# Low parts of 18 token-weight pieces added up by GpSimd's transfers instead of subtracted on VectorE and GpSimd

## The chip, the core and the metric

One NeuronCore of a Trainium2 chip runs the whole program. Its engines are TensorE (PE in the profile; PEld is its weight load), VectorE (DVE), ScalarE (ACT), GpSimd (POOL) and SyncE (SP), which issues all transfers of the kernel before. The metric is the device time of one execution in microseconds (us); lower is better.

## What is computed

The reference is three blocks in a row, on 8 batches of 576 tokens with 512 channels:

```
# attention with keys and values averaged over groups of 8 tokens
attn = softmax(q @ mean8(k).T / 8) @ mean8(v)            # 8 heads of 64
# mixing with a phase
theta = x @ w_theta
y = w_tok_r @ (x * cos(theta)) + w_tok_i @ (x * sin(theta))
u = x + y;  x = u + relu(u @ w_ch)
# token MLP, then channel MLP
u = x + w_tok2.T @ relu(w_tok1.T @ x);  out = u + relu(u @ w_ch1) @ w_ch2
```

The weights arrive in 64-bit floating point. What this case is about is how `w_tok` (the real and the imaginary token weights on top of each other, 9 blocks of 128 rows x 576 columns) becomes two float32r halves for TensorE: a high part, the weight rounded to float32r, and a low part, the weight minus the high part. A product is then high x high + high x low + low x high.

## The kernel before

Batch 0 and the conversion of the weights run side by side in the first 110 us, written by a planner (`first_batches`, class `Plan`). Each operation has one or more ways (engine, estimated ns, a mark, a function), dependencies and homes in SBUF. `Plan.run` simulates the plan once by rank and then in 400 random changes of the priorities with a fixed seed, keeps the best, and emits the operations in that order. After that `Arrange` sorts the instructions of the whole program once more, each engine's on its own, by prices (`price`) and lags (`depend`). So an altered operation or estimate can alter the order of everything around it.

`add_piece` converts one piece. There are 26: pieces 0 to 7 are `w_theta` (256 columns each), pieces 8 to 25 `w_tok`: first the 9 blocks' columns 0 to 287, then their columns 288 to 575. SP loads the 64-bit words into a tile named `early`; ACT writes the absolute value, scaled, into a slot (`absf`, L2254); VectorE shifts it (`shl`, L2258), sets the sign (`sign`, L2262) and the lowest bits (`low3`, L2267), which leaves the weight in fp32. For a token piece ACT then rounds it into the high part (`hi`, L2282), `w()[:, 0]`, and VectorE (for even pieces, `LOWS`) or GpSimd (for odd ones) subtracts the high part into the low part, `w()[:, 1]` (`low`, L2285). The slots are 7 (`mids`: `cvt0`, 3 of `zt1` and 3 of `vr`, seen as cvt and early in the profile); a slot is given back when both `hi` and `low` have read it, and the next `absf` waits for it.

TensorE uses the pieces in the mixing of batch 0: for each half of the channels two groups of columns 0 to 255 (128x256 products) and two of columns 256 to 575 (128x320). A group is 27 products into one bank, `m0` or `m1`: the 9 high parts, the 9 low parts, and the 9 high parts again with the low part of Z. So the last token pieces are wanted when the first 128x320 group begins. A bank is emptied by VectorE (`R<-m`), and the next group of the bank waits for that.

While TensorE would idle before the first mixing product, the planner puts in filler products (`busy`); after it none.

## Time and profile before

| | |
|---|---|
| time, median of 3 runs (lowest to highest) | 1228.55 us (1228.24 to 1229.01) |
| the profiled execution: its time, its span | 1229.43 us, 1227.7 us |
| TensorE busy, instructions | 1218.7 us (99%), 7980 |
| weight loads busy | 1184.0 us (96%) |
| VectorE busy, instructions | 1040.5 us (85%), 1873 |
| ScalarE busy, instructions | 708.2 us (58%), 1467 |
| GpSimd busy, instructions | 320.1 us (26%), 395 |
| transfers | all on SP's queue, 225.42 MB |

The shares are over the whole span. A busy TensorE is one that has a product in flight, and a product that waits in the array counts as busy too, so stretches are better compared by what they contain: so many products of a shape, at the pace that a dense row of them has (the next row's start minus this row's start, over their number), against the time that they took. The granted clock of a stretch, PEclk, is 1.00 at full speed. The records count an fp32 product as two.

### The profile page before, as it was taken

Reading aid. Unit: us, or ns where it says so; the run is one execution under the profiler, and the core shown is the slowest. Engines: PE = TensorE matmul, PEld = TensorE weight load, DVE = VectorE, ACT = ScalarE, POOL = GpSimd, SP = SyncE. Lnnn points to the kernel's source line nnn. Section 1 sums busy time; section 2 is a strip of 40 time slices with the busy share of each in tenths; the row PEclk is TensorE's granted clock in tenths of the full one; section 3 lists DMA queues with packets and bytes.
Section 4 is the critical chain, followed back from the end, with each engine's and each line's share of the span. In section 5 each row is a group of like instructions: output and inputs, shape, how many; then the busy total and the mean of one; then the engine's idle time right before and its main releaser. Section 6 shows DMA issues by size and latency. Waiting matters only on the chain.

```text
span 1227.7 us, 22986 instructions
## 1 busy us (share of the span) xinstructions
PE 1218.7 (99%) x7980; PEld 1184.0 (96%) x7980; DVE 1040.5 (85%) x1873; ACT 708.2 (58%) x1467; POOL 320.1 (26%) x395
## 2 busy tenths in 40 slices
PE   9999999999999999999999999999999999999998
PEld 5889999999999999999999999999999999999998
DVE  7988879899898967999999859889963799998894
ACT  6878776776857664544445456676654543443442
POOL 2152434535253533000012100122100033134113
PEclk9999999999999999999999999999999999999999
DMA  9523335554433466534358887787769867546622
GB/s 332 173 96 125 119 116 159 145 149 128 159 115 97 128 178 206 189 101 130 112 161 227 275 286 247 245 294 258 250 214 330 295 205 251 168 136 225 214 77 77
DMA packets 193556, 226.88 MB, mean 185 GB/s; under 512 B 72992, under 2 KB 147232, under 8 KB 193440
## 3 DMA queue, kind: packets, MB, share of 16 engines
q1 hardware_dynamic: 193440, 225.42, 57.0%
q8 instruction: 63, 1.03, 0.4%
q14 instruction: 53, 0.43, 0.1%
HBM read 140.55 MB, written 84.80 MB: 184 GB/s over the span
## 4 chain that ended last, share of the span: by engine, by line
PE 90%; DVE 4%; DMA 3%; ACT 1%; issue 1%; SPq 0%; POOL 0%; ACTq 0%; DVEq 0%; POOLq 0%
PE m L437 32%; PE x L437 31%; PE t L437 23%; PE x L451 3%; DMA early<-w_tok 1%; DMA con<-consts 1%; DMA raw_n<-scr_x 1%; DMA early<-w_theta 0%; SPq L2160 0%; DVE tmp L2727 0%; DVE early L2267 0%; PE t L451 0%; PE m L451 0%; DMA pool<-pool 0%; DVE early L2262 0%
## 5 line engine op out<-in xcount | busy, mean ns | idle before, releaser
L437 PE MATMUL m<-wtk,Z 128*128 128x320 f32 (+1 forms) x1536 | 254.8, 301 | 1.6 <-ACT wtk L2282 1.4
L437 PEld LDWEIGHTS m<-wtk,Z 128*128 128x128 f32 x1536 | 220.0, 190 | 3.8 <-ACT wtk L2282 2.1
L1901 POOL TENSOR_TENSOR o<-o,u 128x384 f32<-128x384 f32 x12 | 17.6, 1479 | 234.2 <-DVE u L1889 181.1
L1052 POOL TENSOR_TENSOR Z<-tmp,Z 128x1024 fp32r<-128x1024 f32 x26 | 63.2, 2442 | 44.3 <-ACT Z L1051 44.3
L437 PE MATMUL t<-wth,Xh 128*128 128x256 f32 x432 | 60.7, 282 | 0.1
L437 PE MATMUL x<-ope_Xh,wa 128*128 128x384 f32 x288 | 60.2, 337 | 0.0
L437 PE MATMUL x<-ope_Z,wa 128*128 128x384 f32 x300 | 60.0, 337 | 0.0
L437 PE MATMUL m<-wtk,zt 128*128 128x256 f32 (+1 forms) x192 | 57.3, 299 | 0.0
L437 PEld LDWEIGHTS t<-wth,Xh 128*128 128x128 f32 x432 | 55.9, 188 | 0.8 <-DVE tmp L2683 0.3
L437 PE MATMUL x<-ope_Xl,wa 128*128 128x384 f32 x252 | 54.6, 336 | 0.0
L1425 POOL TENSOR_TENSOR wo<-wm,wo 128x256 fp32r<-128x256 f32 (+1 forms) x24 | 17.8, 742 | 138.5 <-ACT wo L1424 121.9
L437 PE MATMUL m<-ope_Z,wa 128*128 128x384 f32 x252 | 53.3, 337 | 0.0
L437 PEld LDWEIGHTS x<-ope_Z,wa 128*128 128x128 f32 x300 | 53.3, 188 | 0.0
L437 PE MATMUL t<-ope_Z,wa 128*128 128x384 f32 x252 | 53.1, 337 | 0.0
L437 PEld LDWEIGHTS x<-ope_Xh,wa 128*128 128x128 f32 x288 | 51.2, 188 | 0.0
L437 PE MATMUL x<-ope_R,wa 128*128 128x384 f32 x240 | 47.3, 337 | 0.3 <-ACT ope_R L1648 0.3
L437 PEld LDWEIGHTS x<-ope_Xl,wa 128*128 128x128 f32 x252 | 44.9, 188 | 0.0
L437 PEld LDWEIGHTS t<-ope_Z,wa 128*128 128x128 f32 x252 | 44.8, 188 | 0.0
L437 PEld LDWEIGHTS m<-ope_Z,wa 128*128 128x128 f32 x252 | 44.6, 188 | 0.0
L437 PEld LDWEIGHTS x<-ope_R,wa 128*128 128x128 f32 x240 | 42.2, 188 | 0.7 <-ACT ope_R L1648 0.6
L437 PE MATMUL x<-bdk,q 128*128 128x144 f32 x292 | 40.9, 287 | 0.0
L437 PE MATMUL x<-opo_Z,wa 128*128 128x384 f32 x216 | 40.6, 336 | 0.0
(476 smaller groups left out, 3634.1 us busy)
## 6 DMA issues: line engine op xcount, KB each, us to landing
wa<-scr_w SPq DMA_DIRECT2D x42, 512.0 KB, 5.3
scr_g<-g SPq DMA_DIRECT2D x108, 192.0 KB, 3.2
scr_u<-R SPq DMA_DIRECT2D x32, 288.0 KB, 2.2
u<-scr_u SPq DMA_DIRECT2D x32, 288.0 KB, 4.4
scr_x<-u SPq DMA_DIRECT2D x32, 288.0 KB, 2.1
raw_n<-scr_x SPq DMA_DIRECT2D x24, 384.0 KB, 4.8
scr_w<-wo SPq DMA_DIRECT2D x36, 256.0 KB, 3.7
o<-scr_x SPq DMA_DIRECT2D x48, 192.0 KB, 3.0
```

The costliest lines, as they stand in the source:

```text
L437: nc.tensor.matmul(out=o, lhsT=l, rhs=r, start=start, stop=stop, skip_group_check=skip)
L451: nc.tensor.transpose(o, i, ident)
L1052: later(1.0 if lo is nc.vector else 0.0, lambda: lo.tensor_sub(out=zl, in0=zv, in1=zh.bitcast(F32)), tg, zg)
L1425: eng.tensor_sub(out=o[:, :, 1], in0=src, in1=o[:, :, 0].bitcast(F32))
L1901: nc.gpsimd.tensor_tensor(out=u22[d].t, in0=u22[d].t, in1=u2[d].t, op=ALU.add)
```

## The change

For the 18 token pieces (`DMAS`) the low part is made otherwise. ACT writes minus the weight into the low part's place (`negative`, which rounds as `hi` does), and GpSimd issues a transfer from the slot to that place which adds what it carries to what stands there (`accumulate`). The slot is given back when `hi` has read it and the transfer has landed. The 9 subtractions on VectorE and the 9 on GpSimd go; 18 ACT instructions and 18 transfers come. The planner is told 1000 ns for the issue and 2500 ns more to the end of such a transfer, `Arrange` 1500 and 3000 ns. These are settings by which it sorts.

```
--- before.py
+++ after.py
@@ -64,6 +64,7 @@
 TRIES = 400
 SEED = 2
 LOWS = range(0, 26, 2)
+DMAS = range(8, 26)
 WS = (1, 2)
 ZL = (1, 1, 1)
 EDVE = (2, 3)
@@ -80,6 +81,7 @@
     SIZE = {"float32": 4, "float32r": 4, "uint32": 4, "bfloat16": 2, "int64": 8}
     TABLE = 1380.0
     LANDING = 1750.0
+    SOFT, SOFT_LANDING = 1500.0, 3000.0
     BEGIN, FIRST, COLD = 750.0, 2600.0, 5000.0
     PACED, LEAD = "ew_", 250e3
     AFTER, MARGIN, RATE, WINDOW = 100e3, 800.0, 300.0, 2500.0
@@ -153,6 +155,8 @@
             return n * 0.833 + (62.0 if ps else 112.0) + (75.0 if len(ins) > 1 else 0.0) + (
                 92.0 if len(outs) > 1 else 0.0), False, table
         if e == "Pool":
+            if op == "DMACopy":
+                return self.SOFT, False, None
             if op == "Memset":
                 return n * 0.9 + 3.0, False, None
             if op == "TensorCopy":
@@ -228,6 +232,8 @@
                 c = self.cost[j]
                 if self.eng[j] == "SP":
                     lag = c[0] + c[1] / (490.0 if c[2] else 262.0) + self.LANDING + self.LAT[e]
+                elif self.eng[j] == "Pool" and self.ins[j].opcode == "DMACopy":
+                    lag = c[0] + self.SOFT_LANDING + self.LAT[e]
                 elif e == "PE" == self.eng[j] and self.acc[i][0][0]["name"] == self.acc[j][0][0]["name"]:
                     lag = c[0]
                 else:
@@ -1962,7 +1968,7 @@
             for o in reversed(self.ops):
                 i = o["i"]
                 e, ns, kb = o["ways"][0][0:3]
-                own = 430.0 + kb * 1024.0 / 262.0 + 1750.0 if e == "SP" else ns + self.TAIL[e]
+                own = 430.0 + kb * 1024.0 / 262.0 + 1750.0 if e == "SP" else ns + self.TAIL[e] + (2500.0 if kb == "dma" else 0.0)
                 self.rank[i] = own + max([0.0] + [self.rank[k] + self.LAT[self.ops[k]["ways"][0][0]] for k in self.after[i]])
 
         def trial(self, prio):
@@ -2041,13 +2047,13 @@
                     if w[2] is True:
                         s = max(s, lock)
                         lock = s + d
-                    elif w[2] and w[2] != table:
+                    elif w[2] and w[2] != "dma" and w[2] != table:
                         s += self.TABLE
                         table = w[2]
                     if e == "PE" and s < 5000.0:
                         d *= 1.7
                     free[e] = s + d
-                    end = s + d + self.TAIL[e]
+                    end = s + d + self.TAIL[e] + (2500.0 if w[2] == "dma" else 0.0)
                 out.append((s, i, w, slot))
                 for g in o["give"]:
                     h = held[id(g)]
@@ -2284,7 +2290,18 @@
             def low(eng):
                 return lambda: eng.tensor_sub(out=w()[:, 1, c0:c1], in0=m_(), in1=w()[:, 0, c0:c1].bitcast(F32))
 
+            def negative():
+                nc.scalar.activation(out=w()[:, 1, c0:c1], in_=m_(), func=ACTF.Copy, scale=-1.0)
+
+            def accumulate():
+                nc.gpsimd.dma_start(out=w()[:, 1, c0:c1], in_=m_(), accum_op=ALU.add)
+
             x = add(("ACT", acs(n), False, hi), [o], hs + [w], give=[hold])
+            if i in DMAS:
+                y = add(("ACT", acs(n), False, negative), [o], hs + [w])
+                y = add(("POOL", 1000.0, "dma", accumulate), [y], hs + [w], give=[hold])
+                conv[what[:3]] = (x, y)
+                return
             ways = [("POOL", po(n), True, low(nc.gpsimd))]
             if i in LOWS:
                 ways = [("DVE", dv(n), True, low(nc.vector))]
```

The order moves with it. GpSimd, from its last softmax copies of batch 0 to the end of the token pieces; `wtk0` to `wtk8` are the blocks, `DMASW` the counters of its own transfers. Before:

```order
L2449 MEMSET vbl_483 128x512 [waits PE_49]
L2285 TENSOR_TENSOR wtk1_485<-early8_359,wtk1_485 128x288 [waits DMAHW2_49,DVE_49,Activation_49]
L2285 TENSOR_TENSOR wtk3_571<-cvt0_287,wtk3_571 128x288 [waits DMAHW6_49,DVE_49,Activation_49]
L2285 TENSOR_TENSOR wtk5_500<-early7_291,wtk5_500 128x288 [waits DVE_49,Activation_49]
L2285 TENSOR_TENSOR wtk7_582<-early8_359,wtk7_582 128x288 [waits Activation_49]
L2285 TENSOR_TENSOR wtk0_542<-early8_359,wtk0_542 128x288 [waits DMAHW0_49,Activation_49]
```

Now, the last eight of the 18 and what follows:

```order
L2297 DMA wtk3_436<-early8_360 128x288 [waits DMASW2_49,Activation_49]
L2297 DMA wtk0_563<-early8_360 128x288 [waits DMASW3_49,Activation_49]
L2297 DMA wtk4_577<-early7_289 128x288 [waits DMASW4_49,Activation_49]
L2297 DMA wtk2_447<-cvt0_285 128x288 [waits DMASW5_49,Activation_49]
L2297 DMA wtk5_528<-early7_289 128x288 [waits DMASW6_49,Activation_49]
L2297 DMA wtk6_569<-early7_289 128x288 [waits DMASW7_49,Activation_49]
L2297 DMA wtk7_572<-early8_360 128x288 [waits DMASW0_49,Activation_49]
L2297 DMA wtk8_567<-early8_360 128x288 [waits DMASW1_49,Activation_49]
L2761 TENSOR_TENSOR Z1_800<-tmp0_771,Z1_800 128x2x512 [waits DMAHW3_49,DMAHW2_49,DMAHW4_49,DMAHW1_49,DMAHW6_49,DMAHW0_49,Activation_49]
```

All 18 transfers stand in GpSimd's one queue ahead of the low parts of Z for the second half.

ScalarE, the last conversions of token pieces. Before, each conversion of a token piece waits for VectorE:

```order
L2254 ACTIVATE early7_291<-early5_252 128x288 [waits DMAHW1_49,DVE_49]
L2282 CAST wtk5_500<-early8_359 128x288 [waits DVE_49]
L2282 CAST wtk0_542<-early8_359 128x288 [waits DVE_49]
L2757 CAST wth2_749<-wt0_390 128x512
L2254 ACTIVATE early8_359<-early6_261 128x288 [waits DMAHW5_49,DVE_49]
L2282 CAST wtk1_485<-early7_291 128x288 [waits DVE_49]
L2282 CAST wtk2_487<-early7_291 128x288 [waits DVE_49]
```

Now (L2260 is `absf`, L2294 `negative`, L2288 `hi`):

```order
L2294 ACTIVATE wtk2_447<-cvt0_285 128x288 [waits DVE_49]
L2294 ACTIVATE wtk5_528<-early7_289 128x288 [waits DVE_49]
L2288 CAST wtk2_447<-cvt0_285 128x288
L2260 ACTIVATE early8_360<-early6_258 128x288 [waits DMAHW5_49,DMASW2_49,Activation_49]
L2294 ACTIVATE wtk6_569<-early7_289 128x288 [waits DVE_49]
L2294 ACTIVATE wtk7_572<-early8_360 128x288 [waits DVE_49]
L2288 CAST wtk5_528<-early7_289 128x288
L2288 CAST wtk6_569<-early7_289 128x288
L2294 ACTIVATE wtk8_567<-early8_360 128x288 [waits DVE_49]
```

`negative` stands ahead of `hi`, and the last piece's `absf` waits for a transfer (DMASW2 is here that of `wtk3`, columns 288 to 575) in place of VectorE.

TensorE, the first 128x320 group. Before, one group runs through alone:

```order
L437 MATMUL m1_764<-wtk7_582,Z0_562 128x320 [waits Activation_49]
L437 MATMUL m1_764<-wtk8_451,zt0_620 128x320 [waits Activation_49]
L437 MATMUL x2_791<-bdk_83,q0_275 128x144 [waits DMAHW7_49,DVE_49,PE_49]
L437 MATMUL x2_791<-bdk_83,q0_275 128x144
L437 MATMUL m1_764<-wtk0_542,Z0_562 128x320 [waits Pool_49]
L437 MATMUL m1_764<-wtk1_485,Z0_562 128x320 [waits DVE_49]
```

Now 17 products of the second group (`m0`) and the scores of batch 1 (`bdk`) stand among the 9 products with low parts, of which these are some:

```order
L443 MATMUL m1_781<-wtk1_504,Z0_565 128x320 [waits DMASW1_49]
L443 MATMUL m0_849<-wtk0_563,Z0_565 128x320 [waits DVE_49]
L443 MATMUL m0_849<-wtk1_504,Z0_565 128x320
L443 MATMUL m1_781<-wtk2_447,Z0_565 128x320 [waits DMASW5_49]
L443 MATMUL x1_810<-bdk_83,q0_292 128x144 [waits DVE_49,PE_49]
L443 MATMUL x1_810<-bdk_83,q0_292 128x144
L443 MATMUL m1_781<-wtk3_436,Z0_565 128x320 [waits DMASW2_49]
```

A low part is thus wanted later than 9 products after its high part.

## Rows read from the trace of the kernel before

**Rows 1.** the windows view: each stretch's busy time by engine, PEclk, DMA share, GB/s.

```profile
53.40:58.80 5.40, 5.40 (x47) 5.40 (x47) 5.27 (x17) 4.05 (x10) 0.00 (x0) 1.00 0.00 0
58.80:61.90 3.10, 3.10 (x11) 1.42 (x10) 3.10 (x9) 2.67 (x7) 2.16 (x2) 1.00 0.00 0
61.90:65.50 3.60, 2.19 (x14) 1.74 (x12) 3.60 (x9) 1.42 (x5) 1.24 (x2) 1.00 0.00 0
...
67.00:69.40 2.40, 2.40 (x12) 2.40 (x11) 2.40 (x4) 1.96 (x4) 0.37 (x1) 0.50 0.37 102
69.40:72.40 3.00, 3.00 (x19) 3.00 (x19) 2.92 (x6) 2.65 (x4) 0.83 (x1) 0.83 0.27 102
```

**Rows 2.** the timeline of TensorE: start, us, instruction, count, idle time and its releaser.

```profile
58.88 3.60 PE L437 MATMUL x<-nat_v,pool 128*128 128x512 f32 x8
61.91 1.44 PE L437 MATMUL m<-wtk,Z 128*128 128x320 f32 x6
...
65.51 0.78 PE L437 MATMUL m<-wtk,Z 128*128 128x320 f32 x2 [1.42 <-ACT wtk L2282]
...
72.49 1.32 PE L437 MATMUL m<-wtk,Z 128*128 128x320 f32 x8
...
73.80 1.03 PE L437 MATMUL m<-wtk,Z 128*128 128x320 f32 x6
74.68 0.90 PE L437 MATMUL x<-bdk,q 128*128 128x144 f32 x6
75.32 0.56 PE L437 MATMUL m<-wtk,Z 128*128 128x320 f32 x2
...
76.25 1.21 PE L437 MATMUL m<-wtk,Z 128*128 128x256 f32 x8
```

**Rows 3.** the instructions of L2285, the subtractions: ns min/median/max, first and last start.

```profile
L2285 DVE TENSOR_TENSOR wtk<-early,wtk x8: 444/451/874, 35.3 to 66.3; 128x288 fp32r<-128x288 f32 x8
L2285 POOL TENSOR_TENSOR wtk<-early,wtk x8: 798/865/1590, 44.7 to 66.4; 128x288 fp32r<-128x288 f32 x8
```

**Rows 4.** the timeline of VectorE around the last pieces.

```profile
52.37 1.24 DVE L2285 TENSOR_TENSOR wtk<-early,wtk 128x288 fp32r<-128x288 f32 x2
...
60.93 0.72 DVE L2267 SCALAR_TENSOR_TENSOR early<-early,early 128x288 uint32<-128x288 uint32 x1
61.57 0.90 DVE L2258 TENSOR_SCALAR early<-early 128x288 uint32<-128x288 uint32 x1
62.39 0.91 DVE L2258 TENSOR_SCALAR cvt<-cvt 128x288 uint32<-128x288 uint32 x1
63.22 0.30 DVE L2258 TENSOR_SCALAR early<-early 128x288 uint32<-128x288 uint32 x1
...
65.29 0.44 DVE L2267 SCALAR_TENSOR_TENSOR early<-early,early 128x288 uint32<-128x288 uint32 x1
65.65 0.67 DVE L2672 SCALAR_TENSOR_TENSOR tmp<-tmp,x 128x512 f32<-128x512 f32 x1
```

**Rows 5.** the timeline of GpSimd at the same place.

```profile
59.74 3.40 POOL L2285 TENSOR_TENSOR wtk<-early,wtk 128x288 fp32r<-128x288 f32 x3 [6.81 <-ACT wtk L2282]
```

**Rows 6.** the timeline of ScalarE: three casts of a token piece in a row.

```profile
45.18 1.09 ACT L2282 CAST wtk<-early 128x288 fp32r<-128x288 f32 x3
```

**Rows 7.** the transfers by issue: count, KB each, median us from issue to landing.

```profile
scr_w<-ew_b SPq DMA_DIRECT2D x48, 128.0 KB, 3.3
...
early<-w_tok SPq DMA_DIRECT2D x14, 288.0 KB, 6.5
...
scr_t<-ew_a SPq DMA_DIRECT2D x5, 128.0 KB, 1.9
```

**Rows 8.** the start: TensorE's fillers and first scores, ScalarE's wait.

```profile
2.30 4.14 PE L447 MATMUL m<-busy 128*128 128x512 bf16 x11 [2.30 <-POOL busy L442]
6.28 1.39 PE L437 MATMUL x<-bdk,q 128*128 128x144 f32 x10
...
14.89 0.95 ACT L2382 ACTIVATE e<-t,mx 128x72 f32<-128x72 f32 x4 [1.96 <-DVE mx L2371]
```

More of the change, by code (lines that the diff above doesn't have):

```diff
@@ L66 @@
 LOWS = range(0, 26, 2)
+DMAS = range(8, 26)
 WS = (1, 2)
@@ L82 @@
     LANDING = 1750.0
+    SOFT, SOFT_LANDING = 1500.0, 3000.0
     BEGIN, FIRST, COLD = 750.0, 2600.0, 5000.0
@@ L155, in price @@
         if e == "Pool":
+            if op == "DMACopy":
+                return self.SOFT, False, None
             if op == "Memset":
@@ L230, in depend @@
                     lag = c[0] + c[1] / (490.0 if c[2] else 262.0) + self.LANDING + self.LAT[e]
+                elif self.eng[j] == "Pool" and self.ins[j].opcode == "DMACopy":
+                    lag = c[0] + self.SOFT_LANDING + self.LAT[e]
                 elif e == "PE" == self.eng[j] and self.acc[i][0][0]["name"] == self.acc[j][0][0]["name"]:
@@ L1964, in prepare @@
                 e, ns, kb = o["ways"][0][0:3]
-                own = 430.0 + kb * 1024.0 / 262.0 + 1750.0 if e == "SP" else ns + self.TAIL[e]
+                own = 430.0 + kb * 1024.0 / 262.0 + 1750.0 if e == "SP" else ns + self.TAIL[e] + (2500.0 if kb == "dma" else 0.0)
                 self.rank[i] = own + max([0.0] + [self.rank[k] + self.LAT[self.ops[k]["ways"][0][0]] for k in self.after[i]])
@@ L2043, in trial @@
                         lock = s + d
-                    elif w[2] and w[2] != table:
+                    elif w[2] and w[2] != "dma" and w[2] != table:
                         s += self.TABLE
@@ L2049, in trial @@
                     free[e] = s + d
-                    end = s + d + self.TAIL[e]
+                    end = s + d + self.TAIL[e] + (2500.0 if w[2] == "dma" else 0.0)
                 out.append((s, i, w, slot))
@@ L2285, in low, with negative, accumulate @@
                 return lambda: eng.tensor_sub(out=w()[:, 1, c0:c1], in0=m_(), in1=w()[:, 0, c0:c1].bitcast(F32))
+            def negative():
+                nc.scalar.activation(out=w()[:, 1, c0:c1], in_=m_(), func=ACTF.Copy, scale=-1.0)
+            def accumulate():
+                nc.gpsimd.dma_start(out=w()[:, 1, c0:c1], in_=m_(), accum_op=ALU.add)
             x = add(("ACT", acs(n), False, hi), [o], hs + [w], give=[hold])
+            if i in DMAS:
+                y = add(("ACT", acs(n), False, negative), [o], hs + [w])
+                y = add(("POOL", 1000.0, "dma", accumulate), [y], hs + [w], give=[hold])
+                conv[what[:3]] = (x, y)
+                return
             ways = [("POOL", po(n), True, low(nc.gpsimd))]
```

## The prediction

> **What bounds the kernel now.** I read the windows first, to find where TensorE is neither idle by name nor at its pace, then TensorE's own timeline there, then VectorE, GpSimd and ScalarE at the same place. The change touches only the first 110 us. The stretch that matters begins when the 256-column groups of batch 0's first half are through, at 58.88, and ends at the first product of the second half, at 76.25: 17.4 us [rows 2]. It holds 8 records of `nat_v` (58.88 to 61.91, 3.03 us), 54 products of 128x320 and 20 records of the scores `bdk` (in four rows, of which one stands in the group). At their dense pace a 320 product takes (73.80-72.49)/9 = 0.146 us (the ninth, of `zt`, has its own row) and a score record (75.32-74.68)/6 = 0.107. That makes 3.03 + 7.88 + 2.14 = 13.05 us. So 4.3 us are lost here, and the windows show as what: TensorE is busy for 2.19 of the 3.60 us from 61.9, with 1.42 of idle time put down to ScalarE's high part, and then the granted clock is 0.50 for 2.4 us and 0.83 for 3.0 [rows 1, 2], which is 1.2 + 0.5 us lost. Behind the high part stands VectorE, busy for all of 58.8 to 65.5 [rows 1]: its `low3` of a last piece ends at 65.65 [rows 4]. Before 58.88 there is little to win: in the window of 5.4 us ahead of it TensorE is busy throughout, with 47 products [rows 1].
>
> **What the change takes from VectorE.** Seven of its nine subtractions lie ahead of the last `low3`: all but the last two, 66.25 and 66.64. Five are spaced 0.37 (the row's next start; a record of 0.45 overlaps the next by 0.08) and two take 1.24, less that overlap 1.16 [rows 3, 4]: 5 x 0.37 + 1.16 = 3.0 us. The nine on GpSimd go too, and they cost VectorE time of its own: beside the three that run from 59.74 for 3.40 us [rows 5], three conversion steps take 0.72, 0.90 and 0.91 where the same steps take 0.44, 0.30 and 0.30 a little later [rows 4]: 1.5 us. Together 4.5 us. The new order gives back some 0.4: two more copies and one reduction come ahead of the pieces, one weight subtraction and one bank's emptying come behind them. So the last `low3` ends near 61.6 instead of 65.65.
>
> **What it adds to ScalarE.** 18 `negative`, priced as the casts of the same tile: three take 1.09, less two overlaps 0.33 each [rows 6], so 5.9 us, half of it in the second half of the pieces. ScalarE is busy for 4.05 + 2.67 + 1.42 = 8.1 of the 12.1 us from 53.4 to 65.5 [rows 1]; 9 x 0.33 = 3.0 us fit into its 4.0 us of idle time, with little to spare. Cover gone, they would stand in the path one for one. In the first half nine more lie between the phases' sines and casts, and I take 0.3 us for what they shift the first mixing group.
>
> **What it adds to GpSimd and to the transfers.** No row of before shows such a transfer. Its issue: below, 0 if it is hidden; above, 1.59, the longest subtraction of that tile on GpSimd; I take 0.8, the shortest one there, as the engine's own price for the tile [rows 3]. From issue to landing: 1.9 is the quickest transfer of a like size, 6.5 what the loads of the pieces take when the queues are full; I take 3.3, the busy middle, since the windows from 53.4 to 65.5 show no transfers at all [rows 1, 7]. Together 4.1 us (1.9 to 8.1). The Trainium skill, DMA: Bandwidth & Descriptors, Anatomy of one DMA, gives about 2.0 us plus bytes / 436e3 for this path, an estimate of 2.3 us for a piece's 147 KB; no row of before shows the path, and by 2.3 the sum would stay as it is.
>
> Who waits for that? TensorE asks for the low parts in the new order. It arrives at the first 320 product at 61.91 + two scores of two records = 62.3. `wtk2`'s low part comes after 13 products and 3 scores: 61.91 + 1.9 + 0.64 = 64.45; `wtk5`'s at 65.75, `wtk8`'s after 34 products and 10 scores at 61.91 + 4.96 + 2.14 = 69.0. VectorE is through with `wtk2` near 58.7, so its `negative` ends at 59.1 and it may take 5.3 us; `wtk8`'s `negative` ends near 62.3 and may take 6.7. At 4.1 both are covered. The slots are the second waiter: the last piece's `absf` waits for the landing of `wtk3`, whose `negative` I put at 55.6: 55.6 + 4.1 = 59.7, and ScalarE would come to it at about 59.7 anyway. So this has no slack: each us above 4.1 moves the last piece, the bank that VectorE empties behind it, and TensorE's first 320 product by one.
>
> **The sum.** Of the 4.3 us all go at 4.1 us per transfer; 0.3 is lost in the first half; and batch 1's softmax, which hangs on the phases of the second half, comes only some 3.5 us sooner (VectorE's part 4.0, minus ScalarE's last `negative`s), so that TensorE gives 0.5 us back there. 4.3 - 0.3 - 0.5 = 3.5; of the rest I expect no change, but take 0.2 off for waits in the new order that I can't see. That is 3.3 us. The profiled execution, 1229.43 (span 1227.7 and 1.7 outside), is 0.9 above the median; the gain is in the span and is taken from the median: 1228.55 - 3.3 = 1225.3.
>
> **Rivals.** (B) The transfer takes the place of the wait. With 6.5 to land and 0.8 to issue it is 7.3: the last piece comes 2.4 us later by the slot (7.3 less 4.1 less the 0.8 that ScalarE has to spare), and as long a wait at the first 320 product costs some clock as it does now, 0.5 us or so. Gain 3.3 - 2.9 = 0.4; with 1.59 to issue, eight in a row on one queue, much the same: 1227.0 to 1228.5. For it: the queue is one, and all 18 stand in it; against: idle transfer engines there.
>
> (C) The issue holds VectorE as the subtractions did. Beside 3.40 us of GpSimd VectorE lost 1.5 us [rows 4, 5], 0.44 us for each. If an issue of 1.59 does the same, the eight last pieces lose 8 x 0.7 = 5.6 us, more than the 4.5 that the change frees; with 0.4 of reordering the last `low3` comes at 67.2 and TensorE waits 1.5 us more at half clock after it: 1228.55 + 1.5 + 0.8 = 1230.9, slower. It decides from 0.56 us lost per issue (4.5 / 8). Against it: an issue has no tile to read.
>
> (D) The plan matters more than the low parts. The same draws now fall on other operations: 14 fillers stand ahead of the first scores where 11 stood, 3 x 0.376 = 1.1 us [rows 8]. I think ScalarE's wait of 1.96 at 14.89 covers it, since the scores of the third pair stand behind it [rows 8]; if not, 1225.3 + 1.1 = 1226.4, and like shifts in the sorting of the other 1100 us could take 1 to 2 us either way: 1224.5 to 1228.5.
>
> (E) VectorE's quick steps hold the issue back. Of the conversion's steps `shl`, at 0.30 where `low3` takes 0.44 on the same tile, moves its elements faster [rows 4]. If an issue can't proceed beside one, each waits at most 0.30, or 0.60 if two follow each other; five issues in a row come 1.5 to 3 us later and the slot's transfer 0.3 to 0.6: 1225.9 to 1227.0. The Trainium skill, SBUF — State Buffer, Who interferes with whom, states such a rule: GpSimd can't write a transfer's descriptors while VectorE runs an instruction in a two-port mode. No row of before shows it, since no transfer is issued there by GpSimd.
>
> **How the numbers follow.** A difference of 0.2% (2.5 us: below 1226.1 or above 1231.0) is about what a measurement of this kernel can tell from no change. The forecast has 0.48 (1224.0 to 1226.5; nine parts in ten of it below 1226.1, 0.43), B 0.21 (1227.0 to 1228.5, but 0.06 of it above 1231.0, where a transfer takes over 9 us and TensorE's wait grows one for one), C 0.13 (0.08 above 1231.0, since an issue may take longer than a subtraction), D 0.12 (0.04 faster, 0.04 slower), E 0.06 (0.02 faster). Faster: 0.43 + 0.04 + 0.02 = 0.49. Slower: 0.06 + 0.08 + 0.04 = 0.18. Same: the other 0.33. The range leaves out the slow ends of B, C and D, 0.18, and hardly anything below, because the stretch holds no more than 4.3 us: 1223.8 to 1231.0.
>
> **What would show it.** In the changed kernel VectorE's last `low3` before 62, its conversion steps at 0.30 and 0.45 throughout; TensorE without a wait of over 0.5 us from 58 to 76 and PEclk at 1.00; the first product of the second half at 72 or sooner. B shows as TensorE or `absf` waiting for a transfer, with 6 us from issue to landing; C as long `shl` and `sign` beside an issue; D as a later first softmax. I am wrong if the last piece is not earlier, or if the stretch is shorter and the time is not.

## The result: 7 us slower, and the profile after

| | before | changed |
|---|---|---|
| median of 6 runs each | 1228.62 us (1227.55 to 1229.65) | 1235.81 us (1235.41 to 1236.49) |
| ratio, 95% interval | | 1.0059 (1.0046 to 1.0072) |
| profiled execution: time, span | 1229.43, 1227.7 us | 1235.89, 1234.1 us |

The forecast was 1225.3, with a range up to 1231.0; the change costs 7.2 us. All of it is lost in the first 106 us. The first `wth` product of batch 1 starts at 98.51 us before and at 105.64 after (last row of the second fence below), 7.1 later; from 150 us on the changed kernel stays some 6 us behind, and its span ends 6.4 later. Before:

```profile
98.51 1.13 PE L437 MATMUL t<-wth,Xh 128*128 128x256 f32 x8
```

The windows, at the stretches of [rows 1] (stretch, its length, busy time and instructions of PE, PEld, DVE, ACT, POOL, then PEclk, DMA share, GB/s):

```profile
53.40:58.80 5.40, 4.86 (x32) 4.06 (x32) 4.88 (x9) 4.49 (x12) 0.88 (x2) 1.00 1.02 248
58.80:61.90 3.10, 0.85 (x5) 0.54 (x4) 1.27 (x3) 0.53 (x2) 1.70 (x2) 0.99 0.95 201
61.90:65.50 3.60, 3.56 (x17) 3.57 (x18) 2.87 (x9) 3.53 (x11) 1.25 (x2) 0.53 0.29 45
65.50:72.40 6.90, 6.90 (x37) 4.99 (x36) 6.56 (x15) 6.76 (x17) 5.00 (x6) 1.00 0.88 133
```

From 58.8 to 61.9 the computing engines are mostly idle: TensorE 0.85 of 3.10 us, VectorE 1.27, ScalarE 0.53, where [rows 1] had TensorE and VectorE at 3.10. What is busy is the transfers: a DMA share of 1.02 and 0.95 where before there was 0.00. From 61.9 to 65.5 TensorE works again, but at a clock of 0.53, near the lower of its two levels (1.2 GHz; 1.00 is 2.4 GHz): that costs 0.47 x 3.56 = 1.7 us. TensorE's timeline tells whom it waits for, as [rows 2] did:

```profile
53.38 0.84 PE L443 MATMUL m<-wtk,Z 128*128 128x256 f32 x3 [1.31 <-ACT wtk L2288]
...
58.51 0.38 PE L443 MATMUL m<-wtk,Z 128*128 128x256 f32 x1 [0.55 <-DMA wtk<-early]
60.36 0.39 PE L443 MATMUL m<-wtk,Z 128*128 128x256 f32 x1 [1.47 <-DMA wtk<-early]
...
61.94 0.58 PE L443 MATMUL m<-wtk,zt 128*128 128x256 f32 x1 [0.82 <-DMA wtk<-early]
...
66.60 3.59 PE L443 MATMUL x<-nat_v,pool 128*128 128x512 f32 x8
...
81.13 1.11 PE L443 MATMUL m<-wtk,Z 128*128 128x256 f32 x8
...
105.64 1.11 PE L443 MATMUL x<-wth,Xh 128*128 128x256 f32 x8
```

Three waits for a low part on its way, 2.84 us together, and they stand in the 256-column groups of the first half, which the forecast thought safe. The `nat_v` products come at 66.60 for 58.88 before, 7.7 later. Of this 5.8 can be named: the 2.84, the 1.31 at 53.38 and the 1.7 of the clock. The stretch behind them that the forecast was about holds the same products as before and is shorter, 81.13 - 66.60 = 14.5 for 17.4 us. That part came about, 2.9 us of it, behind a loss of 7.7. Between 81.13 and 105.64 the changed kernel falls back by 2.2 us more: it has ten 128x320 products more there (1.5 us at 0.146), and waits 0.93 for GpSimd's copies at 95.72.

Now the transfers, which no row of before could show. Three places in the timelines of the changed kernel: GpSimd at the first and at the sixth to eighth transfer; SP's issues of loads; ScalarE and VectorE where they wait for a slot:

```profile
32.40 1.01 POOL L2297 DMA_DIRECT2D wtk<-cvt  x1 [8.85 <-ACT wtk L2288]
...
49.64 1.73 POOL L2297 DMA_DIRECT2D wtk<-early  x2 [0.61 <-ACT wtk L2294]
51.98 0.87 POOL L2297 DMA_DIRECT2D wtk<-early  x1 [0.61 <-ACT tmp L2725]
...
42.51 0.41 SPq L2166 DMA_DIRECT2D kr<-kT  x1
48.75 0.95 SPq L2166 DMA_DIRECT2D nat_v<-v  x2
52.21 0.37 SPq L2166 DMA_DIRECT2D kr<-kT  x1
...
39.23 0.46 ACT L2260 ACTIVATE cvt<-early 128x288 f32<-128x288 f32 x1 [1.49 <-DMA wtk<-cvt]
...
61.96 0.46 ACT L2260 ACTIVATE early<-early 128x288 f32<-128x288 f32 x1 [2.63 <-issue]
...
62.46 0.31 DVE L2264 TENSOR_SCALAR early<-early 128x288 uint32<-128x288 uint32 x1 [2.13 <-ACT early L2260]
...
68.23 0.46 DVE L2273 SCALAR_TENSOR_TENSOR early<-early,early 128x288 uint32<-128x288 uint32 x1
```

Before, SP issued batch 1's `nat_v` earlier:

```profile
42.78 0.95 SPq L2160 DMA_DIRECT2D nat_v<-v  x2
```

From issue to landing (minimum, median, maximum), of the transfer issued at 32.40, of those issued from 49 to 53 (the view counts the one of 48.17 with them, which took the 3.5), and of those from 60 to 72:

```profile
DMA to landing us min/median/max: 6.8/6.8/6.8
...
DMA to landing us min/median/max: 3.5/8.0/8.3
...
DMA to landing us min/median/max: 2.7/2.8/3.1
```

Those without loads beside them land in 2.7 to 3.1 us, near the 3.3 that was taken. The first leaves beside the loads of the pieces and of `q` (DMA share 1.05 from 20 to 35 us) and takes 6.8; `absf` (L2260) waits 1.49 us at 39.23 for its slot. The three of 49.64 to 51.98 leave behind `nat_v`, 1 MB issued at 48.75, and take 7.8 to 8.3. TensorE's first two waits are for the second and the third of these. Its wait of 0.82 is for the next transfer, which is issued only at 57.73 and takes 4.2; by the time at which that lands, 61.89, it also ends the 2.63 us of ScalarE's `absf` at 61.96 (the profile says "issue") and with it VectorE's 2.13. The last `low3` starts at 68.23 for 65.29 before [rows 4]: VectorE has no subtraction left and is later.

Why was that ninth transfer issued so late? The last of the first nine `negative`s ended at 50.87, and GpSimd was idle from 52.85:

```profile
50.10 0.77 ACT L2294 ACTIVATE wtk<-early 128x288 fp32r<-128x288 f32 x2
...
57.73 0.86 POOL L2297 DMA_DIRECT2D wtk<-early  x1 [4.87 <-ACT wtk L2288]
58.78 0.86 POOL L2297 DMA_DIRECT2D wtk<-cvt  x1 [0.19 <-issue]
60.63 0.86 POOL L2297 DMA_DIRECT2D wtk<-early  x1 [0.99 <-issue]
```

The cast that the profile names isn't the reason: in a run below with the same instructions in the same order (e14) the ninth transfer leaves 4.4 us before that cast ends. But the sixth, seventh and eighth transfers landed at 57.42, 58.47 and 60.32, and the ninth, tenth and eleventh left 0.31 us after each of them. The program asks for no such wait: the landings that it makes the ninth wait for had come by 41.72. It is the same everywhere: in the 14 kernels here that have these transfers, none of the 212 was issued while three were on their way, and 84 left 0.25 to 0.31 us after the landing of the third before. So GpSimd's queue took three of them at a time; what sets the three isn't shown. A landing of 8 us thus holds up the issues behind it too, and from the end of its `negative` to its landing the ninth took 11.0 us, where the sum had 4.1.

### The profile page after: what moved, and what is told of

Same layout as the page of the kernel before. It is cut to its first block, busy times and chain, and to the rows that moved or that the text cites. A ratio compares the mean times of both kernels' runs of the same rounds, so it can differ in the third digit from the quotient of the medians.

```text
span 1234.1 us, 23044 instructions
## 1 busy us (share of the span) xinstructions
PE 1220.6 (99%) x7981; PEld 1184.4 (96%) x7981; DVE 1038.8 (84%) x1866; ACT 713.9 (58%) x1480; POOL 329.3 (27%) x407
## 4 chain that ended last, share of the span: by engine, by line
PE 91%; DVE 3%; ACT 2%; issue 1%; POOL 1%; DMA 1%; POOLq 0%; ACTq 0%; DVEq 0%
PE m L443 32%; PE x L443 31%; PE t L443 23%; PE x L457 3%; PE m L453 1%; DMA wtk<-cvt 1%; PE t L457 0%; PE m L457 0%; DMA wtk<-early 0%; POOL e L2429 0%; DVE mx L2388 0%; DVE e L825 0%; ACT e L2399 0%; DVE mx L824 0%; ACT Z L2757 0%
## 5 line engine op out<-in xcount | busy, mean ns | idle before, releaser
L443 PE MATMUL m<-wtk,Z 128*128 128x256 f32 (+1 forms) x1536 | 255.3, 301 | 3.3 <-DMA wtk<-early 2.0
```

The lines of the kernel that those rows point to most:

```text
L443: nc.tensor.matmul(out=o, lhsT=l, rhs=r, start=start, stop=stop, skip_group_check=skip)
```

## First experiments: parts of the change

Theory 1: long landings hold slots and keep TensorE waiting. Theory 2: ScalarE's 18 `negative`. Theory 3: the planner draws another order, and the draw costs the time. The first four kernels each do a part.

Transfers for the second half, or for the first half, only:

```
-DMAS = range(8, 26)
+DMAS = range(17, 26)        # e1_late9
+DMAS = range(8, 17)         # e2_first9
```

> Only the nine pieces of the second half (17 to 25) go through `negative` and the transfer; the first half's nine keep the subtraction. In the trace of the changed kernel the first two transfers, issued at 32.4 and 36.5, took 6.8 and 5.2 us to land beside full queues, ScalarE and VectorE then waited for a conversion slot (1.49 us each at 39), the loads of `kr` and `nat_v` were issued 3.5 to 7.2 us later than before, and transfers 5 to 8 met them. Theory 1 (landings of the first half start the delay): `nat_v` issued at 43 to 45, every landing under 4 us, 1225 to 1229, that is 7 to 10 us less than the changed kernel. Theory 2 (ScalarE's added `negative` costs the time, whatever the landing): half the loss stays, 1231 to 1233. Theory 3 (the order drawn anew, not the transfers): anything from 1226 to 1236, with landings that have nothing to do with it.

> Only the nine pieces of the first half (8 to 16) go through `negative` and the transfer; the second half keeps the subtraction. Theory 1: the first two landings stay at 5 to 7 us, the slots are held at 39, `nat_v` is issued after 47, and most of the loss is here: 1232 to 1236. Theory 2: half the loss, 1231 to 1233, and no wait of TensorE for a landing over 0.5 us matters. If the loss sits in the second half instead (TensorE's waits of 0.55 and 1.47 us for landings at 58.5 and 60.4), the time is 1227 to 1229.

Measured: e1 1231.91 (1.0024, 1.0015 to 1.0032), e2 1233.99 (1.0043, 1.0030 to 1.0056). Each half alone loses, 3 and 5 us. In e1 all nine land in 2.8 to 3.8 us, so its 3 us aren't the landings'.

`negative` kept, and the old subtraction behind it in place of the transfer:

```
 if i in DMAS:
-    y = add(("ACT", acs(n), False, negative), [o], hs + [w])
-    y = add(("POOL", 1000.0, "dma", accumulate), [y], hs + [w], give=[hold])
-    conv[what[:3]] = (x, y)
-    return
+    xn = add(("ACT", acs(n), False, negative), [x], hs + [w])
...
-conv[what[:3]] = (x, add(ways, [x], hs + [w], give=[hold]))
+conv[what[:3]] = (x, add(ways, [xn], hs + [w], give=[hold]))
```

> No transfer: ScalarE still makes the negated high part of all 18 pieces, and then the subtraction of the kernel before overwrites it, on VectorE or GpSimd as there. So ScalarE's added load and the longer chain are there, the issue and the landing are not. Theory 1: the 18 `negative` of 0.33 us cost 0 to 2 us: 1228 to 1231. Theory 2 (ScalarE's load is the cause): 1233 to 1237.

GpSimd's own addition in place of the transfer:

```
-nc.gpsimd.dma_start(out=w()[:, 1, c0:c1], in_=m_(), accum_op=ALU.add)
+nc.gpsimd.tensor_tensor(out=w()[:, 1, c0:c1], in0=w()[:, 1, c0:c1].bitcast(F32), in1=m_(), op=ALU.add)
...
-y = add(("POOL", 1000.0, "dma", accumulate), [y], hs + [w], give=[hold])
+y = add(("POOL", po(n), True, accumulate), [y], hs + [w], give=[hold])
```

> The changed kernel with GpSimd's own addition of the weight to the negated high part in place of the transfer, for all 18 pieces: VectorE makes no subtraction, as in the changed kernel, and nothing lands. Rows of before give 0.8 to 1.59 us for GpSimd's subtraction of that tile, so the low part is there 0.8 to 1.6 us after its `negative` where the landing took 2.7 to 8.3 us after an issue of 0.86. Theory 1: the waits for slots at 39 go, and the time falls to 1226 to 1231. Theory 2: the same ScalarE load, so no better than 1233. A third outcome: GpSimd's 18 additions hold VectorE, as three beside 3.40 us of GpSimd did before, 0.44 us each, and the gain is lost there: 1229 to 1233.

Measured: e3 1231.56 (1.0026, 1.0017 to 1.0035), e4 1235.50 (1.0056, 1.0044 to 1.0069). e4 has no transfer and is as slow as the changed kernel, which looks like the end of theory 1. But the waits are in new places each time. e3's longest, on TensorE, is far behind the pieces:

```profile
117.11 2.08 PE L443 MATMUL t<-wth,Xh 128*128 128x256 f32 x8 [3.05 <-DVE tmp L2699]
```

It waits for VectorE's phases of another batch. (e3's profiled execution took 1234.27, 2.7 above its median, so this wait need not be in most of them.) Every edit had the planner draw its 400 changes over again, so each of these four is a part of the change plus another order. What e4 loses by its additions and what by its order is not settled.

## The order and the work taken apart

The draw by itself, and the transfers in the old order:

```
-SEED = 2
+SEED = 3        # e7_bseed3: the kernel before; e8_seed3: the changed kernel
```

```
# e5_sameplan: the planner sees the subtraction of before, the program gets the transfer
...
+def swap():
+    negative()
+    accumulate()
+ways = [("POOL", po(n), True, swap if i in DMAS else low(nc.gpsimd))]
 if i in LOWS:
+    ways = [("DVE", dv(n), True, swap if i in DMAS else low(nc.vector))]
```

> All 18 transfers, but the planner draws with the kernel before's operations and prices: where it would have placed a subtraction, `negative` and the transfer are issued instead. The planner then knows nothing of the landing nor of ScalarE's 18 extra operations, and the first 150 us are drawn as before; only the pass that sorts the finished program still moves some of them. Theory 1 (landings hold slots, ScalarE and VectorE wait, the loads come late): still slower, 1231 to 1236, with waits for slots or landings of some us in all before 66. Theory 3 (the order drawn anew costs the time, in all runs so far, each in another place): 1226 to 1229.5, since the order is nearly the one of before and the transfers are covered as predicted.

> The kernel before with another seed for the planner's 400 draws (3 for 2); nothing else. It prices the draw alone. Theory 1 and 2, by which operations cost the time: within 1.5 us of before, 1227 to 1230. Theory 3 (the draw): 2 us or more from it, 1231 to 1236, if the seed of before is a good one of many.

> The changed kernel with the same other seed. Theory 1 and 2: within 2 us of the changed kernel, 1234 to 1238, and 5 to 9 us above the kernel before at that seed. Theory 3: anywhere from 1227 to 1238, and no fixed distance to the kernel before at that seed.

Where a run keeps a draw and changes the work in it (e5, e9, e10 and those below), `Arrange` still sorts the finished program by what is in it, so the order that runs is near the other one and not equal to it.

Measured: e5 1229.42 (1.0008, 1.0000 to 1.0017), e7 1234.29 (1.0046, 1.0034 to 1.0059), e8 1232.43 (1.0035, 1.0025 to 1.0046). The kernel before with another seed is 5.9 us slower, and the changed kernel with another seed 3.4 us faster. At seed 3 the changed kernel is the faster one, by 1.9, though the two intervals overlap. Three rows of TensorE in e7:

```profile
67.65 0.79 PE L437 MATMUL m<-wtk,Z 128*128 128x320 f32 x2 [2.60 <-ACT wtk L2282]
...
111.48 0.85 PE L437 MATMUL t<-wth,Xh 128*128 128x256 f32 x5 [1.48 <-ACT Xh L2587]
...
117.52 1.22 PE L437 MATMUL t<-wth,Xh 128*128 128x256 f32 x8 [1.44 <-DVE tmp L2672]
```

So theory 3 seemed to have it: in the old order the transfers cost about 1 us. Then the order drawn for the changed kernel must be slow with any work in it. The test is the other corner, that order with the old subtractions; and seed 3 once more, transfers in the order drawn for the subtractions (e10: e5 with `SEED = 3`):

```
# e9_afterplan: the planner sees negative and the transfer, the program gets neither;
# low() is called where the later of hi and the transfer stood
...
+def both():
+    seen.append(1)
+    if i in DMAS and len(seen) == 2:
+        low(nc.vector if i in LOWS else nc.gpsimd)()
 def negative():
+    pass
 def accumulate():
+    both()
```

> The other corner of the square: the order that the planner draws for the changed kernel, but the work of the kernel before in it. No `negative` is issued, and where the transfer stood (or behind the high part, if that comes later) the subtraction runs, on VectorE for even pieces and on GpSimd for odd ones, as before. The kernel before's work at its own order takes 1228.4 to 1228.7, the transfers at that order 1229.4, the transfers at the new order 1235.8. Theory 3 (the order carries the loss): 1233 to 1238, though no transfer is left. Theory 1 (the transfers carry it, and the order of before only happened to hide them): 1227 to 1231.

> The transfers in the order that the planner draws for the kernel before at seed 3, where the subtractions took 1234.29 and the changed kernel's own draw 1232.43. Theory 3 with a price of about 1 us or less for the swap itself: 1233 to 1236. If the swap gains the 3.3 us that were forecast wherever VectorE ends last (at that seed TensorE waits 2.6 us for the high part before 150 us): 1230 to 1232. Theory 1: 1236 or more.

Measured: e9 1230.04 (1.0012, 1.0003 to 1.0020), e10 1231.87 (1.0028, 1.0019 to 1.0037). As a table of medians:

| order drawn for | subtractions in it | transfers in it |
|---|---|---|
| the subtractions, seed 2 | 1228.6 (before) | 1229.42 (e5) |
| the transfers, seed 2 | 1230.04 (e9) | 1235.81 (changed) |
| the subtractions, seed 3 | 1234.29 (e7) | 1231.87 (e10) |

Theory 3 in the form I had given it falls with e9: the new draw costs the old work 1.3 to 1.4 us. Nor do the transfers as such cost 7: it is 1 us in one order, 5.8 in another, and a gain of 2.4 in a third. TensorE in e9, at the place of the second fence, starts its first 256-column product sooner than 53.38 and waits for nothing up to the `nat_v` products:

```profile
51.60 0.72 PE L443 MATMUL m<-wtk,Z 128*128 128x256 f32 x3
...
59.07 3.59 PE L443 MATMUL x<-nat_v,pool 128*128 128x512 f32 x8
```

Also in e9 `nat_v` is issued late, at 50.07. The late load is thus the order's own choice, and harmless until transfers that somebody waits for leave beside it.

## What the transfers cost in the order drawn for them

Three candidates were left in that order: ScalarE's `negative`, the meeting with `nat_v`, and the slots. Each is changed with the draw held. By the traces e14 has the changed kernel's instructions in its order on every engine but SP; in e13 and e15 `Arrange` moved some on every engine.

e13 is e9 with `negative` issued at its planned place, and the subtraction overwriting it. In e14 the planner is told nothing and batch 1's `nat_v` goes into a home that is free early, so that SP alone issues in another order:

```
 h = vn[b] = home(tag, [128, 5, 512], F32, f"nat_v{b}")
+h.args = ("Xl",) + h.args[1:]        # e14_aftervx
```

e15 keeps the draw with seven slots, but deals the tiles from ten as the program is written down:

```
+ring = [("cvt0", 0)] + [("zt1", x) for x in range(3)] + [("vr", x) for x in range(3)] + [
+    ("n1", 0), ("n1", 1), ("n2", 0)]
...
-tag, k = hold.name()
+box["slot"] = tag, k = ring.pop(0)        # back to the ring after its last reader
```

> The changed kernel's order with its 18 `negative` at their places on ScalarE, but with the subtraction of the kernel before (VectorE for even pieces, GpSimd for odd) overwriting each instead of a transfer. Beside the same order without `negative` (1230.04) it prices ScalarE's part at that order, and the rest of the way to the changed kernel's 1235.8 is the transfers' own. If ScalarE carries it (in the changed kernel it has no idle time from 39.2 to 56.5, and the phases' last cast of `Z` comes at 51.62 for 48.64 without the `negative`): 1233 to 1236. If the landings carry it: 1230 to 1232.

> The changed kernel, but batch 1's `nat_v` is loaded into `Xl`, which is free by then, instead of `R1`, which staged pieces; the planner is told nothing of it, so that TensorE, VectorE, ScalarE and GpSimd have the changed kernel's instructions in its order, one by one. Only SP's order changes: `nat_v` (1 MB) goes out near 35 instead of 48.75, and is no longer on its way beside the transfers issued at 49.6 to 52, which took 7.8 to 8.3 us where quiet ones take 2.7 to 3.1. If that meeting costs TensorE its 2.8 us of waits for landings at 58 to 62: those landings fall to 5 us or less, and the time to 1231.5 to 1234. If the loads beside them matter little, since `kr` and `vlr` stay: 1235 to 1237.

> The changed kernel with its own draw (seven slots as the planner sees them), but when the program is written down the slots are dealt from ten, the longest free first. Near the same order, and no wait for a slot that a landing holds. If the slots cost the time (waits of 1.49 us at 39 and 2.63 at 62 on ScalarE): 1232 to 1234. If ScalarE's load and TensorE's own waits for landings carry it: 1235 to 1237.

Measured: e13 1230.46 (1.0018, 1.0009 to 1.0026), e14 1231.43 (1.0024, 1.0014 to 1.0034), e15 1230.61 (1.0018, 1.0009 to 1.0027). ScalarE's 18 `negative` cost 0.4 us on top of e9's 1230.04, with an uncertainty of about 1 us, so theory 2 is out as the main cause. The early `nat_v` gives back 4.4 of the changed kernel's 1235.81, and e15, with three slots more, 5.2. e14's rows: the landings of the same four transfers as in the changed kernel's view from 49 to 53; then, from the timelines, SP's issue, ScalarE's wait for a slot, and the only wait for weights that TensorE has from 50 to 70:

```profile
DMA to landing us min/median/max: 2.8/3.1/4.8
```

```profile
35.91 1.28 SPq L2166 DMA_DIRECT2D nat_v<-v  x2
...
39.85 0.46 ACT L2261 ACTIVATE cvt<-early 128x288 f32<-128x288 f32 x1 [1.78 <-DMA wtk<-cvt]
...
53.99 0.84 PE L443 MATMUL m<-wtk,Z 128*128 128x256 f32 x3 [1.58 <-ACT wtk L2289]
```

Same instructions, same order, and 8.0 us become 3.1 because the load is out of the way; the three waits for landings are gone. The first transfer still takes 7.1, and the slot is still waited for at 39.85. TensorE's 1.58 at 53.99 stays too; that it comes of that slot is argued from e15, where both are gone, and not shown by itself.

In e15 it is the other way round. The landings of the transfers issued from 44 to 49 are as bad as ever (first fence), but ScalarE is not held at 39, TensorE's first 256-column product starts at 51.32, and its waits for landings from 50 to 60 are three of 0.36 to 0.46. Two more follow, of 0.78 and 0.70:

```profile
DMA to landing us min/median/max: 2.8/7.5/7.9
```

```profile
51.32 0.71 PE L443 MATMUL m<-wtk,Z 128*128 128x256 f32 x3
...
54.97 0.70 PE L443 MATMUL m<-wtk,Z 128*128 128x256 f32 x2 [0.43 <-DMA wtk<-early]
56.03 1.11 PE L443 MATMUL m<-wtk,Z 128*128 128x256 f32 x7 [0.36 <-DMA wtk<-early]
...
58.18 0.86 PE L443 MATMUL m<-wtk,Z 128*128 128x256 f32 x5 [0.46 <-DMA wtk<-early]
...
70.57 0.41 PE L443 MATMUL m<-wtk,Z 128*128 128x320 f32 x1 [0.78 <-DMA wtk<-cvt]
72.72 1.12 PE L443 MATMUL m<-wtk,Z 128*128 128x320 f32 x4 [0.70 <-DMA wtk<-early]
...
55.31 0.46 ACT L2264 ACTIVATE early<-early 128x288 f32<-128x288 f32 x1 [1.68 <-issue]
```

These five waits come to 2.73 us, as much as the changed kernel's 2.84, and ScalarE is held once more at 55.31, just when the transfer issued at 47.62 lands (55.24). So the sum of the waits doesn't tell the time: TensorE reaches its `nat_v` products at 58.88 and not at 66.60. How much of the 5.2 is the slots' stays open, because e15 runs in another order as well: it loads the second `kr` at 64.32 and the three `vlr` from 65.34 on, where the changed kernel loads them at 52.21 and 52.80. Both cures together (e17: e15 with e14's line):

> The changed kernel's draw with both cures: `nat_v` loaded early into `Xl` (alone 1231.43), and slots dealt from ten (alone 1230.61). If the two take away one and the same loss, TensorE's waits for the landings of 8 us: 1229.5 to 1231. If the losses are separate, 4.4 and 5.2 us add up and it ends below the kernel before: 1226 to 1228.5. It ends no lower than that order's own 1230.04 with the subtractions unless the transfers gain something there.

Measured: 1229.43 (1.0006, 0.9997 to 1.0015). Together they give 6.4, less than 4.4 + 5.2: in part they take away one and the same loss. With both, the transfers are level with the subtractions in the same order (1230.04), within the measurement.

Slots without the draw held, and draws that the planner's own reckoning (no time of the chip) calls better:

```
+mids = Slots([("cvt0", 0)] + ... + [("n1", 0), ("n1", 1), ("n2", 0)])    # e6_slots10, seed 2; e11, seed 8
+SEED = 8                                                              # e11_sl10seed8; e12_seed8: seven slots
```

> The changed kernel with ten conversion slots in place of seven (three more in `n1` and `n2`, which nothing else uses so early). Theory 1: the waits for slots at 39 and 62 (1.49 and 2.13 us of VectorE) go, the loads of `kr` and `nat_v` come 3 to 6 us sooner, and the time falls by 3 to 6 us: 1230 to 1233. If the landings themselves, as waits of TensorE, and not the slots, carry the loss: 1234 to 1237. Theory 3: any time from 1228 to 1237, with losses in places where no slot is short.

> Ten slots and seed 8, a draw whose end by the planner's own reckoning is the earliest of the 16 seeds tried at ten slots: 112.6 us where the draws of seed 2 end at 116.2 with ten slots, 116.1 with seven and 115.8 in the kernel before. If that reckoning says what the chip does, 3.6 us below the same slots at seed 2: 1229 to 1231. If it doesn't (at seed 3 the kernel before ended at 115.9 by it and was 5.9 us slower than at seed 2 with 115.8): anywhere from 1227 to 1237.

> The changed kernel, seven slots, at seed 8, where the planner's own reckoning ends at 114.1 us for 116.1 at seed 2. By the reckoning 2 us less than the changed kernel, 1233 to 1235; by theory 3, the draw matters beyond what the reckoning knows: 1227 to 1237. Beside the run before it, it tells what the three slots are worth at one seed: theory 1 gives the ten slots 2 us or more over the seven, as at seed 2.

Measured: e6 1233.71 (1.0042, 1.0030 to 1.0055), e11 1233.84 (1.0043, 1.0031 to 1.0056), e12 1236.47 (1.0065, 1.0052 to 1.0078). With ten slots it takes 2.1 us less at seed 2 and 2.6 less at seed 8; each is a new draw, though, and a draw by itself moved the kernel before by 5.9. The reckoning doesn't order the results: it put e11 3.6 us below e6, and they came out level; it put e12 2 us below the changed kernel, and it is 0.7 above.

## Why the old order gains nothing either

In the order of before the meeting doesn't matter: e5's landings are long too (4.9 to 8.0 us for those issued from 30 to 53), but its trace has no wait for one of them but three of weight loads, 0.7 us together. There the forecast can be checked by itself. e5, the stretches 53.4 to 65.5 of [rows 1], and its last `low3`:

```profile
53.40:58.80 5.40, 5.38 (x32) 3.83 (x30) 5.04 (x15) 5.36 (x16) 4.42 (x5) 1.00 0.84 138
58.80:61.90 3.10, 3.10 (x25) 2.86 (x24) 3.00 (x9) 3.02 (x10) 2.61 (x3) 1.00 0.92 139
61.90:65.50 3.60, 3.48 (x21) 2.72 (x20) 3.50 (x9) 3.51 (x10) 1.89 (x3) 1.00 0.59 87
```

```profile
63.80 0.46 DVE L2273 SCALAR_TENSOR_TENSOR early<-early,early 128x288 uint32<-128x288 uint32 x1
```

TensorE is busy throughout where [rows 1] had 2.19 of 3.60, PEclk is 1.00 and the wait of 1.42 is gone, as forecast. But the last `low3` starts at 63.80, 1.5 us sooner than before and not 4, and ScalarE is busy for 5.36, 3.02 and 3.51 us where it had 4.05, 2.67 and 1.42. The profiled span is 0.7 shorter, the median 0 to 2.1 us longer than before: no gain.

One reason lies in the profile of before itself. Its clock of 0.50 and 0.83 in [rows 1], 1.7 us of the 4.3, belongs to an execution whose mean granted clock over the whole span is 0.999. Of the 112 executions of the kernel before beside these experiments, 62 have 1.000 to three digits, which leaves room for at most 0.6 us lost to the clock, and they are only 0.6 us faster (median 1228.30) than the 46 at 0.999 (1228.86). So holding the clock has less to give than the 1.7 of that one execution.

> The kernel before's order, transfers in the place of the subtractions for the second half's nine pieces alone. With all 18 it took 1229.42, 1.0 above before; there ScalarE was busy for 17.95 of the 18.4 us from 35 to 53.4 and for 18.7 of 19.0 from 53.4 to 72.4, while TensorE's clock held 1.00 from 58.8 to 65.5 as forecast. If ScalarE's nine `negative` in the first half give the gain away: 1226.5 to 1228. If the gain is lost in the second half itself: 1228.5 to 1230.

> The kernel before's order, transfers for pieces 17, 19, 21, 23 and 25 alone, whose subtractions GpSimd made; VectorE keeps its own. VectorE then loses nothing but the stretching beside GpSimd, put at 1.5 us from the rows of before, and ScalarE gets 5 x 0.33 = 1.65 us instead of 3.0. With all nine of the second half (1228.34) ScalarE was busy for 18.8 and VectorE for 18.4 of the 19.0 us from 53.4 to 72.4. If the sum of both engines' work sets the end there, no gain beyond that: 1228 to 1229. If ScalarE alone did: 1226.5 to 1228.

These are e5 with transfers for fewer pieces (`range(17, 26)`, and `range(17, 26, 2)`). Measured: e16 1228.34 (0.9998, 0.9990 to 1.0007), e18 1228.48 (1.0002, 0.9993 to 1.0011). The whole stretch in one window, before and e16:

```profile
53.40:72.40 19.00, 17.58 (x101) 15.08 (x101) 18.79 (x43) 14.08 (x30) 6.06 (x6) 0.91 0.09 29
```

```profile
53.40:72.40 19.00, 18.35 (x122) 15.98 (x121) 18.85 (x39) 18.80 (x42) 10.61 (x12) 1.00 0.47 72
```

TensorE gets 0.77 us more busy time and a clock of 1.00 for 0.91. VectorE is as full as before, 18.85 for 18.79: what the subtractions left was taken by work that stood behind them. ScalarE has gone from 14.08 to 18.80 of 19.0. With both full, TensorE waits for their other work instead, in e16:

```profile
70.52 0.73 PE L443 MATMUL x<-bdk,q 128*128 128x144 f32 x4 [0.55 <-DVE vbl L2483]
...
74.83 1.00 PE L443 MATMUL t<-bdk,q 128*128 128x144 f32 x6 [0.37 <-ACT e L2398]
```

(The expectation of e18 gives VectorE 18.4 us in e16; its row has 18.85, and 18.35 is TensorE's.) From the `nat_v` products (59.40) to the second half's first product (76.13) e16 takes 16.73 us and holds ten score records more than before; at the paces of the prediction that is 13.05 + 10 x 0.107 = 14.1, so 2.6 us are lost where 4.3 were. That 1.7 is about what the profiled span shows (1226.1 for 1227.7), but these two executions lie on opposite sides of their medians (1227.93 for 1228.34, 1229.43 for 1228.55), which makes 1.3 us of it. The medians show no gain, with an interval of 1.2 us less to 0.9 more. e18 leaves ScalarE 1.5 us of idle time there and comes out the same. So it isn't ScalarE alone; that VectorE sets the pace is argued from its 18.6 to 18.9 us, not shown by a run of its own. None of the kernels is under the one of before by more than the measurement can tell.

## The prediction, step by step

- **What bounds before** was right for the profiled execution, and so was what frees it: clock and wait as forecast in e5, and at seed 3, where TensorE waits 2.60 us for the high part, the transfers gain 2.4 us (e10 against e7). But 1.7 of the 4.3 us is the clock of one execution, which more than half of the others don't lose.
- **VectorE's 4.5 us** were too many: the last `low3` came 1.5 us sooner in e5, and 2.4 in e16 (62.89). From 20 us to it, VectorE is busy for 42.23 of 43.80 us in e5 and for 44.59 of 45.29 before: 2.4 us less work stands ahead, since some that stood behind moved up, and it idles 0.9 more. The sum had 0.4 for this.
- **ScalarE's 5.9 us**, "half hidden", with 0.3 us for the first half: 0.4 us in all in the new order (e13, less than its uncertainty). What was not seen is that ScalarE is then full in the old order (18.80 of 19.0 us in e16).
- **The issue**, 0.8: 0.85 to 0.88 for most. The longer ones, 1.20 in the changed kernel, begin while the issue before is still running (50.18 in one that ends at 50.49) and end 0.88 after it. Right as a price; what the sum lacked is that an issue can have to wait for a landing.
- **The landing, 3.3, and with it the 4.1 from `negative` to landing, is the step that failed.** It rested on "the windows from 53.4 to 65.5 show no transfers at all". That holds for the old order. In the new one `nat_v` is issued at 48.75 instead of 42.78, and eight of the transfers leave before 53.4, where the old profile had loads as well. Four of the eight took 6.8 and 7.8 to 8.3 us, above the bound of 6.5, taken as it was from loads that leave when the queues are full; the other four took 2.7 to 5.2. Then the ninth could not be issued before the sixth had landed, so that its 4.1 became 11.0. The nine transfers of the first half got no landing of their own at all. With the one load of `nat_v` moved away 4.4 of the 7.2 us come back (e14). The other 2.8 are less certain: 1.3 to 1.4 is what the new draw costs the old work (e9).
- **The slots**: "this has no slack: each us above 4.1 moves the last piece" was right and was applied to one piece. In the changed kernel landings hold `absf` for its slot three times, 1.49, 0.57 and 2.63 us. What ten slots give by themselves is open (e15).
- **Rival B** named the mechanism, "TensorE or `absf` waiting for a transfer, with 6 us from issue to landing", and priced it for one slot and one wait, 1227.0 to 1228.5. It came in the first half, with three waits and three held slots; e14 and e17 put it at 4.4 to 6.4 of the 7.2 us.
- **Rival D**, the plan: 1 to 2 us either way. The draw alone cost the old work 1.3 to 1.4 (e9), which is inside; but another draw moves the same kernel by 5.9 us (e7), and it is the draw that put the load beside the transfers.
- **Rivals C and E** didn't come: conversion steps last 0.30 and 0.45 us beside an issue as elsewhere, and an issue 0.86. One `shl` of 0.96 at 33.16 stands beside GpSimd's fill of `vbl` (33.12, 0.83 us), as one of 0.65 did before. The Trainium skill, SBUF — State Buffer, Who interferes with whom, would have GpSimd's descriptor writing held back by VectorE's quick steps; the rows don't show it: also the longest issues, 1.20 us (the changed kernel) and 1.56 (e5), end 0.9 after the issue before them.

## What to carry to other kernels

A resource's idle time in the profile of before is no promise where the edit lets a planner draw again: price a new transfer at the landing of a full queue wherever any load can be moved beside it, and give the buffers that it holds enough depth for that. Ask also how many such transfers the issuing queue takes at a time, since one that lands late holds up the issues behind it. Before judging an edit in a program that is ordered by a search, measure the search's own spread with another seed, and separate order from work by building the old work in the new order and the new work in the old. Moving time from one full engine to a half idle one gains only until the second is full, so look for what stands behind the freed work. And compare the profiled execution with the others' time and clock before its losses go into a sum.

## What the chip showed that was not expected

A transfer of 144 KB that GpSimd issues and that adds in flight, SBUF to SBUF, took 2.7 to 3.1 us from issue to landing without loads beside it and, in the changed kernel, 6.8 and 7.8 to 8.3 behind loads that SP had issued; the same transfers, in the same instruction order, went from 8.0 to 3.1 (medians of those issued from 49 to 53) when one load of 1 MB was moved. The Trainium skill, DMA: Bandwidth & Descriptors, Anatomy of one DMA, gives a fixed cost plus bytes over a rate for this path, an estimate of 2.3 us; the quiet ones come near it, and behind loads those of the changed kernel take up to 6.0 us more.

GpSimd's queue took at most three of these transfers at a time: of the 212 in the 14 kernels none was issued sooner than 0.25 us after the landing of the third before it, and 84 within 0.31.
